# Routing attention and a bilinear feed-forward layer on one core: eight small moves in a hand-written order of work

## The chip, the cores and the metric

The kernel runs on one core of a Trainium2 chip. A core has five engines, each with its own instruction stream that it works through in order: TensorE (PE in the profile, with the loading of its weights as PEld), VectorE (DVE), ScalarE (ACT), GpSimd (POOL) and SyncE (SP, which here only issues DMAs). Work on one engine waits for work on another through semaphores. The metric is the device time of one execution in microseconds (us).

## What is computed

Attention with routing (4 batches, 8 heads, 768 positions, 64 wide, 16 centroids to a head), and a feed-forward layer on its output (3072 tokens, 512 wide, 1536 inside):

```python
q_n, k_n, c_n = (t / (norm(t) + 1e-6) for t in (q, k, centroids))
q_assign = argmax(einsum('bhsd,hcd->bhsc', q_n, c_n))
k_assign = argmax(einsum('bhsd,hcd->bhsc', k_n, c_n))
mask = q_assign[:, :, :, None] == k_assign[:, :, None, :]
scores = where(mask, q @ k.T / sqrt(64), -1e9)
x = softmax(scores) @ v               # regrouped to (3072, 512)
out = ((x @ w_a) * (x @ w_b)) @ w_out # weights come as 64-bit floats
```

## The kernel before, in words

**Attention.** Two heads of one batch make a *pair* p (0 to 15; HP = 4 pairs to a batch, so that pair 4 is the first of batch 1). A pair has two halves hf of 384 query positions, a half has six key blocks j, and one key block of one half is a *unit*. The loop at the end of `short_path` runs over *groups* g of two units: six groups to a pair, 96 in all, and l = g % 6 is the group's place in its pair. In each group the following is issued, in this order: the scores of group g (`score`: TensorE L556, then the exponential on ScalarE, L565); the sums of the exponentials of the group before, which become the softmax's denominators (`add_up`, L586, on VectorE or GpSimd); the last step of a weight's rounding (`flush_w`, L302, VectorE); the products with v of the group before (`weigh`, L597); in every third group the products that sum the denominators across partitions (`denominators`, L620, copied out by ScalarE, L625); one preparing step of the next pair (`ready[l]()`); the rounding of a weight (`round_w`, four VectorE instructions L280 to L290, then GpSimd L295), where one is due; and then as many *pieces* of the feed-forward layer as a credit allows. After each piece one entry of the list `todo` is issued, and then another rounding if one is due. What is left in `todo` comes at the end of the group.

**What `todo` holds.** Small VectorE steps: a half's normalisation (`normalize`: transposition L640, reciprocal L643, transposition L647, and the product L652 that scales x, which is on GpSimd), and for pairs from 4 on (`by_blocks`) the steps of the next pair's routing. These are, by l: the transpositions of q and k (L477), the transposition of the similarities out of the accumulator that `prep_sim` has just filled (L481; the products are TensorE L373), the maxima (L502 to L507), the one-hots (L487 on GpSimd, L489 on VectorE) and their transposition (L493). Once the feed-forward layer has begun, so from pair 5's preparation (g = 25) on, the accumulator of `prep_sim` is one of the two that the next group's scores need (`apart()`).

**The feed-forward layer.** Batch 0 is computed with plain products (`ffn_block`): its first 8 pieces, which need x of pair 3's first half, are put into the list `ffn` at g = 22. Batches 1 to 3 use a scheme of seven products in place of eight (`ffn_ups`, then `ffn_downs`). It needs sums and differences of blocks of x (`combine_x`, L755, six VectorE instructions; `combine_t4`, L767) and of the weights (`combine`, L782: S1, S2 as `half_1`, S3, S4 as `half_2`, two instructions each). A *part* is one block of one weight: the products p1, p2, p6, p5, p7, p3, p4 in this order, 12 parts to a batch. Every product has eight matmuls (L678), and its result is added up by VectorE (`add`, L815; L864 in p4) or copied by ScalarE (`take`, L812). A part uses three accumulators X, Y and Z; the next part's Y is the same accumulator as this one's, so the next part's p2 has to wait until this part's p3 has been added up. `half_1` of the next part is issued after p7's own steps, and `half_2` after p4's. The last products of `ffn_downs` add up their results at L939. `combine_x` is put into `ffn` in front of the last two of these (`FREE_ROOM` = 2); the next batch's p1 and p2 follow them.

**The beginning.** 24 matmuls at L1053 and 12 transpositions of the identity (`keep_busy`, L332) run while the first q and k arrive. Pair 0's twelve blocks of q and k are transposed in three calls i = 0, 1, 2 of `prep_transpose` (L354), and copied out of the accumulators by VectorE (L360, L363) or ScalarE (L361, L365). In between, the centroids are transposed (L321) and copied (L322, L325), and `prep_sim(0)` (L373) needs them.

Of the kernel before, what the change touches and what calls it, by code (L numbers as in the profile page):

```python
# [14 lines left out]
ALU = mybir.AluOpType  # L15
# [123 lines left out]
def short_path(nc, tc, ctx, c, cn, centroids_in, casts, n_far, q, k, v,  # L139
# [3 lines left out]
    B, H, S, D = q.shape  # L143
# [3 lines left out]
    HP = H // 2  # L147
# [3 lines left out]
    HB = S // 2  # L151
# [177 lines left out]
    def keep_busy(n):  # L329

        for _ in range(n):
            nc.tensor.transpose(out=idle[:, 0:P], in_=ident, identity=ident)  # L332
# [15 lines left out]
    def prep_transpose(p, i):  # L348
        if i == 0:
            qkTs[p] = qtp.tile([P, 2 * S], FP32, name="qkT")  # L350
        ps = ps_m.tile([P, 512], FP32, name="m")
        for n in range(4):
            w, j = divmod(4 * i + n, NJ)
            nc.tensor.transpose(  # L354
                out=ps[:, n * P:(n + 1) * P],
                in_=qks[p][:, w, j].rearrange("p a d -> p (a d)"),
                identity=ident)
        dst = qkTs[p][:, i * 512:(i + 1) * 512]
        if p == 0 and i == 2:
            nc.vector.tensor_copy(out=dst[:, 0:256], in_=ps[:, 0:256])  # L360
            nc.scalar.copy(out=dst[:, 256:], in_=ps[:, 256:])  # L361
        elif p == 0 and i != 1 or p == 1 and i == 2:
            nc.vector.tensor_copy(out=dst, in_=ps)  # L363
        else:
            nc.scalar.copy(out=dst, in_=ps)  # L365
# [148 lines left out]
    def prep_steps(p):  # L514
        if p >= NPAIR:
            return [lambda: None] * 6

        def both(*fs):
            return lambda: [f() for f in fs]

        if by_blocks(p):
            steps = prep_by_blocks(p)
            ready = [lambda s=s: todo.extend(s) for s in steps]
            ready[1] = both(lambda: prep_sim(p), lambda: load_v(p), ready[1])
            return ready

        return [
            lambda: p > 1 and (prep_transpose(p, 0), prep_transpose(p, 1)),
            both(lambda: prep_sim(p), lambda: load_v(p)),
            lambda: todo.extend(prep_assign(prep_across(p))),  # L530
            lambda: None,
            lambda: prep_onehot(p, 1),
            lambda: None,
        ]
# [41 lines left out]
    def add_up(u):  # L576
        p, hf, j = where(u)
        if j == 0 or j == NJ - 1 and p < HP:
            return
        if j == 1:  # L580
            accs[p, hf] = accp.tile([P, 2, HB], FP32, name="acc")
        acc = accs[p, hf]
        for a in range(2):
            many = p >= HP and (a == 1 or j in (2, 4))
            eng = nc.gpsimd if many else nc.vector
            eng.tensor_tensor(  # L586
                out=acc[:, a, :],
                in0=probs[u - 1][:, a, :] if j == 1 else acc[:, a, :],
                in1=probs[u][:, a, :], op=ALU.add)
# [39 lines left out]
    def normalize(p, hf):  # L629

        b, hp = divmod(p, HP)
        acc = den_of.pop((p, hf))
        den, once = acc[:, 0, :], acc[:, 1, :]
        x = xTs[b][:, hp, hf * HB:(hf + 1) * HB]
        inv = small.tile([P, HB // 32], FP32, name="inv")

        def across():
            nc.vector.transpose(out=once, in_=den)  # L640

        def invert():
            nc.vector.reciprocal(  # L643
                out=inv, in_=once.rearrange("p (j t) -> p j t", t=32)[:, :, 0])

        def back():
            nc.vector.transpose(  # L647
                out=den,
                in_=inv[:, :, None].broadcast_to((P, HB // 32, 32)))

        def apply():
            nc.gpsimd.tensor_tensor(out=x, in0=x, in1=den, op=ALU.mult)  # L652
            unchecked.append((4 * p + 2 * hf + 1, inv))

        return [across, invert, back, apply]
# [88 lines left out]
                      chunks(comb.rearrange("p (c f) -> p c f", c=2)),  # L744
                      [t[:, HB:] for t in size]]

    def combine_x(b):
        up_room()
        x = xTs[b]
        for c in range(2):  # L750
            x11, x12 = x[:, c, 0:HB], x[:, c, HB:S]
            x22 = x[:, c + 2, HB:S]
            t2, t3 = W["T2"][c], W["T3"][c]
            for out, l, r in ((t3, x22, x12), (x12, x12, x11), (t2, x22, x12)):
                nc.vector.tensor_tensor(out=out, in0=l, in1=r, op=ALU.subtract)  # L755

    def ffn_ups(b, h):

# [11 lines left out]
        def products(w_sb, i, is_a):  # L770
# [11 lines left out]
                    nc.vector.tensor_tensor(out=dst[c], in0=l[c], in1=r[c], op=op)  # L782
                A[name] = dst

            def half_1():
                combine("S1", A["21"], A["22"], ALU.add)
                combine("S2", A["S1"], A["11"], ALU.subtract)

            def half_2():
                combine("S3", A["11"], A["21"], ALU.subtract)  # L790
                combine("S4", A["12"], A["S2"], ALU.subtract)
                s = W["slots"]
                W["slots"] = [s[0], s[2], s[1], s[3]]
# [70 lines left out]
                nc.vector.tensor_tensor(out=to, in0=to, in1=box["X"][:, 0:HB],  # L864
                                        op=ALU.mult)

            return half_1, half_2, [p1, p2, p6, p5, p7, p3, p4]

        parts = [products(w_sb, i, w_sb is wa_sb) for i in range(NF // 2)
                 for w_sb in (wa_sb, wb_sb)]  # L870
        pieces = []
        for n, (half_1, half_2, ps) in enumerate(parts):
            if n == 0:
                ps[0] = both(half_1, half_2, ps[0])
                ps[2] = both(combine_t4, ps[2])
            if n + 1 < len(parts):
                ps[4] = both(ps[4], parts[n + 1][0])
                ps[6] = both(ps[6], parts[n + 1][1])
            pieces += [(2 * HB, f) for f in ps]
        return pieces  # L880

# [124 lines left out]
    def both(*fs):  # L1006
        return lambda: [f() for f in fs]
# [3 lines left out]
    def ffn_ready(p, hf):  # L1011

        b, hp = divmod(p, HP)
        if hp < HP - 1:
            return
        if b > 0:
            if hf == 0:
                return
            h = []
            ffn.insert(len(ffn) - FREE_ROOM, (0, lambda: combine_x(b)))  # L1020
            ffn.extend(ffn_ups(b, h) + ffn_downs(b, lambda: h))
        elif hf == 0:
            blocks[0] = ffn_block(0, 0)
            ffn.extend(blocks[0][0][0:8])
        else:
            ups0, box0 = blocks[0]
            ups, box = ffn_block(0, 1)
            for n in range(3):
                ffn.extend(ups[8 * n:8 * n + 8] + ups0[8 * n + 8:8 * n + 16])
            ffn.extend(ffn_downs(0, lambda: (box0["h"], box["h"])))  # L1030
# [21 lines left out]
    for _ in range(12):  # L1052
        nc.tensor.matmul(out=idle[0:D, 0:D], lhsT=ones, rhs=ones, start=True,  # L1053
                         stop=True)
    keep_busy(12)
    prep_transpose(0, 0)
    prep_transpose(0, 1)
    centroids_across()
    prep_transpose(0, 2)
# [24 lines left out]
    for g in range(NG + 3):  # L1084
        p, l = divmod(g, GPP)
        if l == 0:
            ready = prep_steps(p + 1)
        now = (2 * g, 2 * g + 1)
        before = (2 * g - 2, 2 * g - 1)
        if g == 1:  # L1090
            weigh(before)
        if 0 < g < NG:
            score(now)
        check_inverses()
        if 0 < g <= NG:
            for u in before:
                add_up(u)
        flush_w()
        if 1 < g <= NG:
            weigh(before)  # L1100
        late = int(g > EARLY)
        if g % 3 == late and 0 < g - late:
            denominators(*divmod(g // 3 - 1, 2))
        if g < NG:
            ready[l]()
        parts = due.get(g, [])

        def round_next():
            if parts:
                i = parts.pop(0)  # L1110
                round_w(i)
                load_w(i + 2)

        round_next()
        if g <= EARLY:
            first, second = 4, 1
        else:
            first, second = 5, 3 if g < NG else 2
        ph = {first: (p, 0), second: (p - 1, 1)}.get(l)
        halved = ph in den_of  # L1120
        if halved:
            todo.extend(normalize(*ph))
        if ffn:
            credit += PER_GROUP[(g > 2 * BG + 3) + (g > 3 * BG + 3)]
            least = FREE_ROOM if halved and ph[1] and (ph[0] + 1) % HP == 0 else 0
            while len(ffn) > least and credit > 0:
                cost, piece = ffn.popleft()
                credit -= cost
                piece()
                if todo:  # L1130
                    todo.popleft()()
                round_next()
        else:
            credit = 0
        round_next()
        while todo:
            todo.popleft()()
        if halved:
            ffn_ready(*ph)
        if l == 0 and p + 1 < NPAIR:  # L1140
            if p and not by_blocks(p + 1):
                prep_transpose(p + 1, 2)
            load(p + 2)
        if l == 4 and p + 1 < NPAIR and not by_blocks(p + 1):
            prep_onehot(p + 1, 0)
# [248 lines left out]
```

## Time and profile before

| what | value |
|---|---|
| median of nine runs | 1048.04 us (1047.7 to 1048.74) |
| the profiled execution | 1047.8 us |
| its span, first to last instruction | 1045.6 us |
| mean granted TensorE clock | 0.999 |
| TensorE busy | 1033.0 us, 99% |
| VectorE busy | 657.2 us, 63% |
| GpSimd busy | 329.8 us, 32% |
| ScalarE busy | 303.2 us, 29% |
| chain that ended last | PE 93%, DVE 4%, issue 1%, POOL 1% |

The span lies within the execution's time; the 2.2 us between them lie around it. "Busy" counts instructions that run or wait in the engine's pipe: for TensorE the end of a matmul is modelled, so that a short pause between matmuls can hide in it. In the timeline a line gives start, length, engine, line of code, operation, output and inputs, the number of merged instructions, and in brackets how long the engine had been idle before and what released it.

### The profile page before, as it was taken

To read this page: it belongs to the slowest core of one execution; us is meant where nothing else is said; L and a number is where in the kernel's file an instruction comes from. 1 tells how busy PE (TensorE), PEld (TensorE's weight loads), DVE (VectorE), ACT (ScalarE), POOL (GpSimd) and SP (SyncE) were. 2 spreads that over 40 slices of the span, in tenths; PEclk is the share of its full clock that TensorE was granted. 3 is DMA by queue.
4 is the path that set the end of the run, shared out by engine and by line. 5 is a ranking of instruction groups with operands and counts; after the bars stand their busy time and mean duration, and the time that the engine had idled before them with its cause. 6 is when DMAs were issued, how large, how long until landed. Compare 5 with 4: busy or idle time off the path is not lost.

```text
span 1045.6 us, 17833 instructions
## 1 busy us (share of the span) xinstructions
PE 1033.0 (99%) x7163; PEld 502.7 (48%) x7163; DVE 657.2 (63%) x1314; ACT 303.2 (29%) x590; POOL 329.8 (32%) x311
## 2 busy tenths in 40 slices
PE   9999999999999999999999999999999999999997
PEld 5444444444445554444444555444444565444565
DVE  6778877887857447555556746755454845554652
ACT  5665333233322222333322122233232201111100
POOL 1111345455543323343442422443333310211100
PEclk9999999999999999999999999999999999999999
DMA  7334243526230120203020030300000000000001
GB/s 183 87 86 86 85 107 105 122 70 145 63 50 18 41 44 22 39 5 46 4 46 2 25 67 24 47 1 20 1 4 1 11 31 21 1 1 1 1 31 34
DMA packets 120521, 46.48 MB, mean 44 GB/s; under 512 B 106608, under 2 KB 115824, under 8 KB 120432
## 3 DMA queue, kind: packets, MB, share of 16 engines
q1 hardware_dynamic: 120016, 44.85, 18.8%
q8 instruction: 58, 0.95, 0.4%
q10 hardware_dynamic: 416, 0.43, 0.1%
q14 instruction: 31, 0.25, 0.1%
HBM read 37.78 MB, written 6.29 MB: 42 GB/s over the span
## 4 chain that ended last, share of the span: by engine, by line
PE 93%; DVE 4%; issue 1%; POOL 1%; ACT 0%; DMA 0%; DVEq 0%; POOLq 0%
PE m L678 62%; PE s L556 15%; PE O L597 12%; PE s L620 1%; PE s L373 1%; PE m L620 1%; DVE raw L755 1%; PE m L373 0%; POOL xT L652 0%; DMA h<-in_q_dram 0%; DVE xT L755 0%; PE m L354 0%; DVE comb L782 0%; DVE acc L586 0%; DVE acc L647 0%
## 5 line engine op out<-in xcount | busy, mean ns | idle before, releaser
L565 ACT ACTIVATE pt<-s 128x768 f32<-128x768 f32 x192 | 145.3, 808 | 206.5 <-PE s L556 165.0
L586 POOL TENSOR_TENSOR acc<-acc,pt 128x384 f32<-128x384 f32 x144 | 152.5, 1073 | 60.2 <-ACT pt L565 43.0
L597 PE MATMUL O<-pt,v 128*64 128x384 f32 x768 | 145.0, 499 | 0.0
L556 PE MATMUL s<-qkT 64*128 64x384 f32 x768 | 139.7, 482 | 0.0
L821 POOL TENSOR_TENSOR h<-h,ha 128x384 f32<-128x384 f32 x54 | 55.4, 1029 | 258.7 <-DVE ha L815 257.8
L678 PE MATMUL m<-xT,wa_sb 128*64 128x384 f32 x672 | 117.5, 487 | 2.8 <-DVE ha L815 1.0
L678 PE MATMUL m<-xT,wb_sb 128*64 128x384 f32 x672 | 116.9, 487 | 0.0
L815 DVE TENSOR_TENSOR ha<-ha,m 128x384 f32<-128x384 f32 x72 | 39.6, 550 | 98.0 <-PE m L678 75.4
L586 DVE TENSOR_TENSOR acc<-acc,pt 128x384 f32<-128x384 f32 x96 | 74.5, 802 | 36.5 <-POOL acc L586 35.5
L815 DVE TENSOR_TENSOR h<-h,m 128x384 f32<-128x384 f32 x72 | 39.5, 549 | 80.8 <-PE m L678 53.9
L812 ACT COPY h<-m 128x384 f32<-128x384 f32 x72 | 34.5, 479 | 184.9 <-PE m L678 184.9
L597 PEld LDWEIGHTS O<-pt,v 128*64 128x64 f32 x768 | 46.7, 136 | 85.8 <-issue 80.1
L678 PE MATMUL m<-wo_sb,h 128*64 128x256 f32 x768 | 86.7, 379 | 0.0
L556 PEld LDWEIGHTS s<-qkT 64*128 64x128 f32 x768 | 70.5, 187 | 31.3 <-issue 0.2
L678 PEld LDWEIGHTS m<-xT,wa_sb 128*64 128x64 f32 x672 | 48.7, 137 | 63.4 <-issue 53.3
L678 PE MATMUL m<-raw 128*64 128x384 f32 x432 | 78.9, 486 | 0.0
L652 POOL TENSOR_TENSOR xT<-xT,acc 128x384 f32<-128x384 f32 x32 | 32.9, 1027 | 144.9 <-DVE acc L647 144.8
L678 PEld LDWEIGHTS m<-xT,wb_sb 128*64 128x64 f32 x672 | 49.0, 137 | 60.1 <-issue 56.1
L678 PEld LDWEIGHTS m<-wo_sb,h 128*64 128x64 f32 x768 | 55.0, 137 | 31.0 <-issue 5.0
L678 PE MATMUL m<-xT,h 128*64 128x256 f32 x576 | 64.5, 379 | 0.0
L678 PE MATMUL m<-xT,size 128*64 128x384 f32 x288 | 52.7, 487 | 0.0
L678 PEld LDWEIGHTS m<-xT,h 128*64 128x64 f32 x576 | 41.4, 137 | 22.3 <-issue 2.3
(169 smaller groups left out, 1302.3 us busy)
## 6 DMA issues: line engine op xcount, KB each, us to landing
raw<-in_moe_w_a_dram SPq DMA_DIRECT2D x12, 512.0 KB, 3.9
raw<-in_moe_w_b_dram SPq DMA_DIRECT2D x12, 512.0 KB, 3.7
raw<-in_moe_w_out_dram SPq DMA_DIRECT2D x12, 512.0 KB, 3.7
qk<-in_q_dram SPq DMA_DIRECT2D x48, 96.0 KB, 3.1
qk<-in_k_dram SPq DMA_DIRECT2D x48, 96.0 KB, 3.6
v<-in_v_dram SPq DMA_DIRECT2D x24, 192.0 KB, 3.9
out_dram<-rest SPq DMA_DIRECT2D x24, 128.0 KB, 1.7
v<-in_v_dram SPq DMA_DIRECT2D x4, 384.0 KB, 4.5
```

The costliest lines, as they stand in the source:

```text
L373: nc.tensor.matmul(out=ps[32 * kq:32 * kq + 32, 0:HB], lhsT=cTb[:, hp, :], rhs=qkTs[p][:, kq * HB:(kq + 1) * HB], start=True, stop=True)
L556: nc.tensor.matmul(out=s[:, a, 0:HB], lhsT=Ts[p][r, S + j * P:S + (j + 1) * P], rhs=Ts[p][r, hf * HB:(hf + 1) * HB], start=start, stop=not ...
L565: nc.scalar.activation(out=pt, in_=s[:, :, 0:HB], func=AF.Exp, scale=SCALE)
L586: eng.tensor_tensor(out=acc[:, a, :], in0=probs[u - 1][:, a, :] if j == 1 else acc[:, a, :], in1=probs[u][:, a, :], op=ALU.add)
L597: nc.tensor.matmul(out=O_of[0][a * D:(a + 1) * D, 0:HB], lhsT=vs[p][:, a, j, :], rhs=probs[u][:, a, :], start=(j == 0), stop=(j == NJ - 1))
L620: nc.tensor.matmul(out=ps[a * D:(a + 1) * D, 0:HB], lhsT=ones, rhs=t[:, a, :], start=(n == 0), stop=(n == len(terms) - 1))
L652: nc.gpsimd.tensor_tensor(out=x, in0=x, in1=den, op=ALU.mult)
L678: nc.tensor.matmul(out=ps[half], lhsT=lhsT[:, half], rhs=rhs, **kw)
L755: nc.vector.tensor_tensor(out=out, in0=l, in1=r, op=ALU.subtract)
L812: nc.scalar.copy(out=box[name], in_=box["X"][:, 0:HB])
L815: nc.vector.tensor_tensor(out=box[name], in0=box[name], in1=box[bank][:, 0:HB], op=ALU.add)
L821: nc.gpsimd.tensor_tensor(out=to, in0=to, in1=box[name], op=ALU.mult)
```

## The change

Eight edits, in the order of the code:

1. The first pair's copies: i = 0 goes from VectorE to ScalarE, and i = 2, which the two engines shared, goes to VectorE alone. (Pair 1 keeps its copies.)
2. The similarities' transposition (L481) leaves `todo` and is issued at once, after `prep_sim` and the load of v.
3. Of a half's sums for a = 0, VectorE does j = 1, 2, 3 and GpSimd j = 4, 5; before, VectorE did j = 1, 3, 5 and GpSimd j = 2, 4. The sums for a = 1 stay on GpSimd.
4. The scaling of x for pair 3's first half is done by VectorE and no longer by GpSimd.
5. `combine_x` is cut into two pieces of three instructions; the second is put between the last two products of `ffn_downs`.
6. The combinations of weights come in three steps: S1 after p7, S2 after p3, S3 and S4 after p4.
7. Of the 12 `keep_busy` transpositions at the beginning, 5 stay, and 2 come after the first call of `prep_transpose`.
8. The denominators of pair 3's second half are put into `ffn`, behind the first piece of group 24.

```diff
-        if p == 0 and i == 2:
-            nc.vector.tensor_copy(out=dst[:, 0:256], in_=ps[:, 0:256])
-            nc.scalar.copy(out=dst[:, 256:], in_=ps[:, 256:])
-        elif p == 0 and i != 1 or p == 1 and i == 2:
+        if p < 2 and i == 2:
             nc.vector.tensor_copy(out=dst, in_=ps)
         else:
             nc.scalar.copy(out=dst, in_=ps)
...
-            ready[1] = both(lambda: prep_sim(p), lambda: load_v(p), ready[1])
+            ready[1] = both(lambda: prep_sim(p), lambda: load_v(p), steps[1][0],
+                            lambda: todo.extend(steps[1][1:]))
...
-            many = p >= HP and (a == 1 or j in (2, 4))
+            many = p >= HP and (a == 1 or j > 3)
...
-            nc.gpsimd.tensor_tensor(out=x, in0=x, in1=den, op=ALU.mult)
+            eng = nc.vector if (p, hf) == (HP - 1, 0) else nc.gpsimd
+            eng.tensor_tensor(out=x, in0=x, in1=den, op=ALU.mult)
...
-    def combine_x(b):
-        up_room()
+    def combine_x(b, c):
+        if c == 0:
+            up_room()
         x = xTs[b]
-        for c in range(2):
...
-            def half_1():
+            def first():
                 combine("S1", A["21"], A["22"], ALU.add)
+
+            def second():
                 combine("S2", A["S1"], A["11"], ALU.subtract)
 
-            def half_2():
+            def others():
...
-                ps[4] = both(ps[4], parts[n + 1][0])
-                ps[6] = both(ps[6], parts[n + 1][1])
+                for i, step in enumerate(parts[n + 1][0], 4):
+                    ps[i] = both(ps[i], step)
...
-            ffn.insert(len(ffn) - FREE_ROOM, (0, lambda: combine_x(b)))
+            for c in range(2):
+                ffn.insert(len(ffn) - FREE_ROOM + c, (0, lambda c=c: combine_x(b, c)))
...
-    keep_busy(12)
+    keep_busy(5)
     prep_transpose(0, 0)
+    keep_busy(2)
     prep_transpose(0, 1)
...
-            denominators(*divmod(g // 3 - 1, 2))
+            half = divmod(g // 3 - 1, 2)
+            if half == (HP - 1, 1):
+                ffn.insert(1, (0, lambda: denominators(HP - 1, 1)))
+            else:
+                denominators(*half)
```

More of the change, by code (lines that the diff above doesn't have):

```diff
@@ L745, in up_room @@
                       [t[:, HB:] for t in size]]
-    def combine_x(b):
-        up_room()
+    def combine_x(b, c):
+        if c == 0:
+            up_room()
         x = xTs[b]
-        for c in range(2):
[L751 to L755, printed above, removed]
+        x11, x12 = x[:, c, 0:HB], x[:, c, HB:S]
+        x22 = x[:, c + 2, HB:S]
+        t2, t3 = W["T2"][c], W["T3"][c]
+        for out, l, r in ((t3, x22, x12), (x12, x12, x11), (t2, x22, x12)):
+            nc.vector.tensor_tensor(out=out, in0=l, in1=r, op=ALU.subtract)
     def ffn_ups(b, h):
@@ L865, in p4 @@
                                         op=ALU.mult)
-            return half_1, half_2, [p1, p2, p6, p5, p7, p3, p4]
+            return (first, second, others), [p1, p2, p6, p5, p7, p3, p4]
         parts = [products(w_sb, i, w_sb is wa_sb) for i in range(NF // 2)
@@ L871, in ffn_ups @@
         pieces = []
-        for n, (half_1, half_2, ps) in enumerate(parts):
+        for n, (combinations, ps) in enumerate(parts):
             if n == 0:
-                ps[0] = both(half_1, half_2, ps[0])
+                ps[0] = both(*combinations, ps[0])
                 ps[2] = both(combine_t4, ps[2])
             if n + 1 < len(parts):
-                ps[4] = both(ps[4], parts[n + 1][0])
-                ps[6] = both(ps[6], parts[n + 1][1])
+                for i, step in enumerate(parts[n + 1][0], 4):
+                    ps[i] = both(ps[i], step)
             pieces += [(2 * HB, f) for f in ps]
```

## The prediction

> **What bounds the kernel.** I read the page's shares first, then TensorE's waits, then the timeline around each.
>
> ```profile
> PE 1033.0 (99%) x7163; PEld 502.7 (48%) x7163; DVE 657.2 (63%) x1314; ACT 303.2 (29%) x590; POOL 329.8 (32%) x311
> ```
>
> TensorE is the bound. No edit removes any of its matmuls but five idle transpositions, so a gain can only be time in which TensorE waits. Its waits, all but the first 1.1 us and three small ones of the start:
>
> ```profile
> PE m L678 <- DVE ha L815: 1.0, 2, 0.5
> PE s L556 <- DVE sim L481: 1.0, 1, 1.0
> PE m L678 <- POOL xT L652: 0.9, 1, 0.9
> PE m L678 <- DVE rest L939: 0.9, 2, 0.4
> PE m L373 <- DVE cTb L325: 0.6, 1, 0.6
> PE s L620 <- DVE acc L586: 0.5, 1, 0.5
> ```
>
> Total, times, longest. They are idle time after a modelled end, so the loss is larger. I measure it by starts: the chain of waits has 32 L678 matmuls in 5.16 us, 0.161 each; a run of n that is followed later than n x 0.161 has lost the rest.
>
> **The change part by part.**
>
> *Combinations of x in two parts (5).*
>
> ```profile
> 396.54 0.57 DVE oh L493
> 397.11 0.32 DVE rest L939
> 397.42 0.04 issue
> 397.47 1.51 PE m L678 x8
> ```
>
> This is the chain that ended last. p1 starts at 395.57, p2 could at 396.86 and does at 397.47: 0.61 lost, because the last products' sum (L939) stands behind six L755 (390.24 to 396.6). With three ahead (to 392.9, then L493, 0.57) it runs at about 393.5, right after its product's end (393.15). The other three, 2.4 us at most beside GpSimd's sums, end near 396.2, and the next L939 near 396.6; its accumulator is wanted only after p2 and p6. The same at 646.42 (0.60); batch 3 loses nothing there. **-1.2 us**.
>
> *Combinations of weights one at a time (6).*
>
> ```profile
> 505.67 1.31 DVE L782 TENSOR_TENSOR comb<-wa_sb 128x128 f32<-128x128 f32 x2
> ...
> 508.43 0.54 DVE L815 TENSOR_TENSOR ha<-ha,m 128x384 f32<-128x384 f32 x1
> ...
> 509.02 1.51 PE L678 MATMUL m<-xT,wa_sb 128*64 128x384 f32 x8 [0.51 <-DVE ha L815]
> ```
>
> In the timeline, p1 of the next part starts at 507.05, so p2 could start at 508.34: 0.68 lost, as at 757.97. p3's sum (508.43) is behind S1, S2 (506.91 to 508.04) and a one-hot (L489). With S2 behind it, it starts 1.05 earlier, at 507.4, and ends at 507.95; what is next is 0.35 us of slack. S2 is wanted by p6, a product later and two attention steps on. **-1.35 us**.
>
> *Denominators behind a product (8).* From 122.07 to the scores at 129.78 TensorE has 40 matmuls (6.45 us, 0.1 for the change of kind) and takes 7.71: 1.16 lost, since acc is only summed at 123.3 and the two halves of the array then run out of step until 129.4. A product of 2.58 in front covers that. Its accumulator is free; the exit copy (L625) is over long before the next scores. **-1.15 us**.
>
> *Similarities put across at once (2)* has two sides.
>
> ```profile
> 136.64 0.56 DVE L709 TENSOR_TENSOR h<-ha,m 128x384 f32<-128x384 f32 x1 [3.66 <-PE m L678]
> 137.11 0.58 DVE L481 STREAM_TRANSPOSE sim<-s 128x384 f32<-128x384 f32 x1
> ...
> 137.75 0.34 PE L556 MATMUL s<-ohT 64*128 64x384 bf16 x2 [0.95 <-DVE sim L481]
> ```
>
> The gain: at g = 25 the scores wait for L481, which waits behind a piece's product. A pair of L556 in bf16 takes 0.17, and the first started at 136.46, so TensorE could go on at 136.63: 1.12 lost. The similarities are there at 133.8, and VectorE is idle for 3.66 us before 136.64: L481 then ends near 134.4, two microseconds before the scores. Rounding (2.25, below) moves behind it and ends about when L709 is due. **-1.1 us**.
>
> The loss: `ready[l]()` comes before `round_next()`, so L481 now stands *in front of* a due rounding and holds it until the similarities exist. At g = 19 this matters:
>
> ```profile
> 95.83 0.58 DVE L481 STREAM_TRANSPOSE sim<-m 128x384 f32<-128x384 f32 x1 [2.41 <-PE m L373]
> ...
> 101.98 1.02 DVE L586 TENSOR_TENSOR acc<-acc,pt 128x384 f32<-128x384 f32 x2
> 102.59 1.33 PE L620 MATMUL m<-acc,ones 128*64 128x384 f32 x4
> ```
>
> TensorE's L373 runs from 94.91; before 95.83 VectorE is idle for 2.41 us, with the rounding done from 91.09 to 93.42. The rounding falls behind 96.34; its price is the step of the same four instructions from 104.91 to 107.16, 2.25 us. From 95.83 on VectorE has no pause (11.63 busy of 12.20 us from 95.8 to 108), so L586 comes at 104.2, and the denominators, which already lose 0.45 here (two waits of 0.23), lose 2.25 more. GpSimd's L295 and the one-hots queue behind it, all as late. **+2.25 us**. At g = 31 the same order costs VectorE 1.1 us of waiting (free at 191.08, similarities done 192.2), and L709 still meets its product's end: nothing. Bounds for this edit's later pairs: from no loss to 2.25 for g = 37 as well; taken: none.
>
> *Scaling on VectorE (4).* Piece 1 starts at 110.07; its 12 matmuls end at 112.00, the rest wait until 113.05 for L652 on GpSimd: 1.05 lost. VectorE's product of this shape takes 0.55 (L586, 0.56 for one) and follows L647 (ends 111.70) with no handover; GpSimd's took 0.17 to begin and 1.13. So x is there near 112.3. It moves L586 of the next sums back by 0.5, which the missing contention returns (four took 2.73 there, two take 1.02). **-0.7 us**, bounded by -1.05 (the whole wait) and 0 (the handover is no dearer than VectorE's queue); the late chain of g = 19 shifts both sides alike.
>
> *VectorE's sums first (3).* The same number of sums on each engine. VectorE loses its waits on GpSimd (DVE acc L586 <- POOL acc L586: 35.5 us, 18 times), none on TensorE's path. GpSimd has two sums in a half's middle group and four in the last, 4.3 us against 3.2. Denominators come a group later: the closest is 849.86, 3.52 after the last sum (846.34); 2.4 stay. **0**; bounds: -0.5 (a sum of p3 that gets clear) to +2 (three places like 509.02).
> [...]
>
> *First pair (1, 7).* The chain runs q's landing, VectorE's chain for the centroids, L322, L325, L373. Without i = 0's copy L322 starts at 7.11, when L321 has ended, not 7.20. The last L373 waits now for ScalarE's half of i = 2 (8.47 to 8.85, starts at 8.90); VectorE alone copies from 7.93 to 8.62 (0.69, row of L363), so it starts at 8.66. ScalarE is free for i = 0 at 6.23 and for i = 1 at 6.85. **-0.2 us**; bounds -0.6 (TensorE's wait for L325) to +1.4: the idle transpositions run at two paces, three of L332 from 3.83 to 4.53 (0.23 apart), twelve of L354 at 40.87 in 1.46 (0.12); if the change of pace came late, the first pair's 13 would cost 0.11 more each.
> [...]
>
> **Sum.** -1.2 - 1.35 - 1.15 - 1.1 + 2.25 - 0.7 - 0.2 = -3.45. From the profiled 1047.8 (0.24 under the median of 1048.04): 1044.35, say **1044.4 us**.
>
> **Rivals.**
> - *The late rounding is caught up* (g = 19): if VectorE's order lets L586 through, -5.7: 1042.1. For it: only the code's order says otherwise. Against: no idle time on VectorE until 107.7.
> - *VectorE's lag goes on* into the first pieces: it is 13.56 busy of 16 us from 114 to 130. Then the denominators and the scores of g = 26 wait for it still, and 2.25 of gains go: 1046.6. Against: denominators want acc near 126.8, and with 2.1 us of lag it is there at 125.5.
> - *The start misses its pace*: +1.4 and no -0.2: 1045.9, on the border.
> - *Slower: GpSimd's four sums hold up p3's sum.* Place: L782 and one step of `todo` between p7's sum and p3's. With ScalarE's copy 0.7, L815 0.55, S1 1.31, a step at 1.36 and L815 0.55 the chain has 4.46 us for three products, 3.87: 0.6 a part. Six of 36 parts eat the gain; from ten on it is slower. Twelve: 1044.4 + 7.2 = 1051.6. For it: two places did this before. Against: S2's 0.5 to 1.1 has left that chain.
> - *It does nothing*: TensorE's short waits come back at the next accumulator. That has the lag's price.
>
> **Numbers.** Forecast 0.55, caught up 0.12, lag 0.18, pace 0.08, slower 0.07. 0.2% of 1048.04 is 2.1 us, about what a measurement can tell from none: faster is under 1045.9. The forecast, the first rival and a part of the pace's make 0.71; same, with the lag and the pace's rest, 0.22; slower 0.07. The range leaves out the slower rival and the edges: 1042.0 to 1047.0.
>
> **What would show it.** Right: no wait on L939, L652's is gone or 0.3, none on L481; p2 straight behind p1; one new wait of TensorE at L620 near 102 us, for VectorE's acc, of about 2.3; L280 behind L481 at g = 19. Wrong: that wait absent, new waits of L678 for L815, or L620 waiting for GpSimd.

## The result, and the profile after

The changed kernel takes 1044.98 us, the median of 10 runs (1043.89 to 1045.6), against 1048.07 for the kernel before in 30 runs (1047.39 to 1048.87). The ratio is 0.9968, 95% interval 0.996 to 0.9976: faster by 3.1 us, where 3.6 was forecast. The profiled execution took 1043.79 with a span of 1042.1, 4.0 less than the profiled 1047.8 of before.

One thing has to be known about these times: they have two levels. Six of twelve executions had a mean granted TensorE clock of 0.997 and average 1045.26; six had 0.998 or more and average 1044.00. The profiled one is of the second kind. Why there are two levels is one of the findings below.

First the shares on the page:

```profile
span 1042.1 us, 17904 instructions
...
PE 1030.8 (99%) x7158; PEld 500.1 (48%) x7158; DVE 658.8 (63%) x1314; ACT 303.0 (29%) x590; POOL 334.1 (32%) x310
```

The span fell by 3.6, and TensorE has the same instructions but for the five idle transpositions, so the gain is waiting time. (Its busy time fell by 2.2, since a short pause between matmuls counts as busy.) TensorE's waits (total, times, longest):

```profile
PE m L619 <- DVE acc L585: 2.1, 1, 2.1
PE O L1057 <- DVE ones L80: 1.1, 1, 1.1
PE m L370 <- DVE cTb L325: 0.5, 1, 0.5
PE m L447 <- DVE oh L421: 0.4, 2, 0.3
PE m L679 <- DVE raw L910: 0.3, 1, 0.3
PE m L447 <- ACT qkT L362: 0.3, 1, 0.3
PE m L679 <- DVE xT L653: 0.2, 1, 0.2
```

The waits for L815, L481, L652's scaling on GpSimd and L939 are gone (L939 is L942 now, L815 is L818). Two are new: 2.1 for `acc` at L619, which was forecast, and 0.3 for L910, which was not; the 0.2 for L653 is what is left of the wait for the scaling. The timeline around the first:

```profile
94.40 0.85 PE L370 MATMUL m<-qkT,cTb 128*32 128x384 f32 x8
95.32 0.58 DVE L478 STREAM_TRANSPOSE sim<-m 128x384 f32<-128x384 f32 x1 [4.66 <-PE m L370]
95.82 0.39 DVE L280 TENSOR_SCALAR wa_sb<-raw 128x512 int32<-128x512 int32 x1
...
103.72 1.02 DVE L585 TENSOR_TENSOR acc<-acc,pt 128x384 f32<-128x384 f32 x2
104.32 1.33 PE L619 MATMUL m<-acc,ones 128*64 128x384 f32 x4 [2.10 <-DVE acc L585]
```

VectorE stands idle for 4.66 us before the similarities' transposition (2.41 before the change), with the due rounding (L280) behind it, and pays that back at 103.72, where TensorE waits. Three of the gains, each as one line of the timelines: VectorE's scaling of x with the wait that is left, the product moved in front of p2 of the next part, and p3's sum (L818) in front of S2 (the L783 behind it).

```profile
114.08 0.87 PE L679 MATMUL m<-xT,wa_sb 128*64 128x384 f32 x4 [0.17 <-DVE xT L653]
...
393.91 2.75 PE L679 MATMUL m<-xT,wa_sb 128*64 128x384 f32 x16
...
505.13 0.54 DVE L818 TENSOR_TENSOR ha<-ha,m 128x384 f32<-128x384 f32 x1
505.60 0.66 DVE L783 TENSOR_TENSOR raw<-comb,wa_sb 128x128 f32<-128x128 f32 x2
```

p1 and p2 at 393.91 are one run of 16 matmuls without a gap; before, the second eight followed 0.61 late.

**Where the time went, by steps.** TensorE works through a fixed list, so I take the start of each group's scores (the first L556 of group g, now L554) in both profiles and look where the difference changes:

| place | before | after | step | edit, forecast |
|---|---|---|---|---|
| g = 0, counted from the first L227 | 6.22 | 6.00 | -0.22 | 1 and 7: -0.2 |
| g = 22 | 103.85 | 105.58 | +2.25 | 2: +2.25 |
| g = 24 | 119.01 | 120.04 | -0.70 | 4: -0.7 |
| g = 25 | 129.78 | 129.65 | -1.16 | 8: -1.15 |
| g = 27 | 151.06 | 149.81 | -1.13 | 2: -1.1 |
| g = 38 | 255.2 | 253.54 | -0.40 | none |
| g = 53 and 77 | 398.91, 647.86 | 396.6, 644.82 | -0.66, -0.65 | 5: -1.2 |
| g = 64 and 88 | 510.46, 759.41 | 507.42, 755.64 | -0.73, -0.73 | 6: -1.35 |
| g = 71 | 581.99 | 579.6 | +0.65 | 3: 0 |

In this execution L227, which waits for q's landing, itself came 0.28 earlier. With that and 0.2 lost at the very end the steps make the span's 3.57. The time outside the span is 1.7 instead of 2.2; that gives the other 0.5 of the profiled difference.

### The profile page after: what moved, and what is told of

Same layout as the page of the kernel before. It is cut to its first block, busy times and chain, and to the rows that moved or that the text cites. A ratio compares the mean times of both kernels' runs of the same rounds, so it can differ in the third digit from the quotient of the medians.

```text
span 1042.1 us, 17904 instructions
## 1 busy us (share of the span) xinstructions
PE 1030.8 (99%) x7158; PEld 500.1 (48%) x7158; DVE 658.8 (63%) x1314; ACT 303.0 (29%) x590; POOL 334.1 (32%) x310
## 4 chain that ended last, share of the span: by engine, by line
PE 95%; DVE 2%; issue 1%; POOL 0%; DMA 0%; ACT 0%; DVEq 0%; POOLq 0%
PE m L679 63%; PE s L554 15%; PE O L596 13%; PE s L619 2%; PE m L619 1%; PE s L370 1%; PE m L370 0%; PE m L354 0%; DMA h<-in_q_dram 0%; DVE xT L910 0%; DVE raw L910 0%; PE m L430 0%; POOL xT L653 0%; PE m L384 0%; DVE h L919 0%
## 5 line engine op out<-in xcount | busy, mean ns | idle before, releaser
L585 POOL TENSOR_TENSOR acc<-acc,pt 128x384 f32<-128x384 f32 x144 | 155.6, 1101 | 60.0 <-ACT pt L563 45.9
L554 PE MATMUL s<-qkT 64*128 64x384 f32 x768 | 139.7, 483 | 0.0
L824 POOL TENSOR_TENSOR h<-h,ha 128x384 f32<-128x384 f32 x54 | 56.0, 1040 | 255.6 <-DVE ha L818 255.2
L818 DVE TENSOR_TENSOR ha<-ha,m 128x384 f32<-128x384 f32 x72 | 39.7, 551 | 106.5 <-PE m L679 80.4
L815 ACT COPY h<-m 128x384 f32<-128x384 f32 x72 | 34.5, 479 | 184.9 <-PE m L679 181.5
L554 PEld LDWEIGHTS s<-qkT 64*128 64x128 f32 x768 | 70.5, 187 | 31.3 <-issue 0.2
L818 DVE TENSOR_TENSOR h<-h,m 128x384 f32<-128x384 f32 x72 | 39.5, 549 | 72.3 <-PE m L679 46.9
L653 POOL TENSOR_TENSOR xT<-xT,acc 128x384 f32<-128x384 f32 x31 | 32.4, 1046 | 143.1 <-DVE acc L646 143.1
L585 DVE TENSOR_TENSOR acc<-acc,pt 128x384 f32<-128x384 f32 x96 | 63.4, 687 | 2.3 <-ACT pt L563 1.0
```

Source lines behind the costliest of these rows:

```text
L554: nc.tensor.matmul(out=s[:, a, 0:HB], lhsT=Ts[p][r, S + j * P:S + (j + 1) * P], rhs=Ts[p][r, hf * HB:(hf + 1) * HB], start=start, stop=not ...
L585: eng.tensor_tensor(out=acc[:, a, :], in0=probs[u - 1][:, a, :] if j == 1 else acc[:, a, :], in1=probs[u][:, a, :], op=ALU.add)
L653: eng.tensor_tensor(out=x, in0=x, in1=den, op=ALU.mult)
L815: nc.scalar.copy(out=box[name], in_=box["X"][:, 0:HB])
L818: nc.vector.tensor_tensor(out=box[name], in0=box[name], in1=box[bank][:, 0:HB], op=ALU.add)
L824: nc.gpsimd.tensor_tensor(out=to, in0=to, in1=box[name], op=ALU.mult)
```

## The experiments

Each edit is to the changed kernel unless another is named. "Step" is the difference as in the table.

**The sums' order (3).** `e1_sums_back` undoes edit 3 alone:

```diff
-            many = p >= HP and (a == 1 or j > 3)
+            many = p >= HP and (a == 1 or j in (2, 4))
```

> The changed kernel with edit 3 undone: VectorE sums j = 1, 3, 5 again and GpSimd j = 2, 4. Theory: the new loss of 0.65 us of TensorE before the scores of group 71 comes from GpSimd's four sums in a row, which hold VectorE's one-hot (0.55 us before, 1.21 after); undone, the loss goes, and the 0.40 us gained before the scores of group 38 (VectorE free earlier for the transposition of q and k) goes too: 0.25 us faster, at most 0.7. Rival: the loss at group 71 comes from the order of the pieces; it stays, and the kernel is 0.4 us slower.

1044.76 us (1044.47 to 1045.94, 7 runs), ratio to before 0.9971 [0.996, 0.9982]. In medians nothing shows, but three steps move: 0.65 comes back at g = 71, 0.79 is lost at g = 38 and 0.14 at g = 32. By the steps e1 is 0.28 slower than the changed kernel, where 0.25 faster was expected. (The 0.79 is more than the 0.40 that the whole change gains there; e5, below, says where the rest is from.)

The gain at g = 38 begins one group earlier. Before the change, VectorE waits for GpSimd's sum (L586); from there it has no pause until the transposition of q and k (L477), and the second half of TensorE's L373 waits for that:

```profile
241.84 1.34 DVE L586 TENSOR_TENSOR acc<-acc,pt 128x384 f32<-128x384 f32 x1 [2.10 <-POOL acc L586]
247.23 1.83 DVE L477 STREAM_TRANSPOSE qkT<-qk 128x768 f32<-128x768 f32 x2
248.70 1.25 PE L373 MATMUL s<-qkT,cTb 128*32 128x384 f32 x8
249.11 0.14 PEld L373 LDWEIGHTS s<-qkT,cTb 128*32 128x32 f32 x4 [0.27 <-DVE qkT L477]
```

In the changed kernel VectorE does not wait there, the transposition (L474) ends before L370 begins, and L370 has no pause:

```profile
244.96 1.82 DVE L474 STREAM_TRANSPOSE qkT<-qk 128x768 f32<-128x768 f32 x2
247.44 0.85 PE L370 MATMUL s<-qkT,cTb 128*32 128x384 f32 x8
```

What happens at g = 71 is on VectorE too. In the changed kernel's timeline GpSimd does this:

```profile
559.66 3.88 POOL L585 TENSOR_TENSOR acc<-acc,pt 128x384 f32<-128x384 f32 x4
563.62 1.04 POOL L484 TENSOR_TENSOR oh<-sim,first 64x384 bf16<-64x384 f32 x1
```

VectorE in the same stretch, and 12 us on:

```profile
562.75 1.21 DVE L486 TENSOR_TENSOR oh<-sim,first 64x384 bf16<-64x384 f32 x1
...
574.55 3.98 DVE L910 TENSOR_TENSOR raw<-wo_sb 128x512 f32<-128x512 f32 x3
```

And TensorE, with the wait at its end:

```profile
578.58 1.08 PE L679 MATMUL m<-raw,ha 128*64 128x256 f32 x8 [0.32 <-DVE raw L910]
```

And VectorE of `e1_sums_back` at the same one-hot and the same L910:

```profile
562.28 1.34 DVE L585 TENSOR_TENSOR acc<-acc,pt 128x384 f32<-128x384 f32 x1 [2.10 <-POOL acc L585]
564.40 0.54 DVE L486 TENSOR_TENSOR oh<-sim,first 64x384 bf16<-64x384 f32 x1
...
575.85 3.69 DVE L910 TENSOR_TENSOR raw<-wo_sb 128x512 f32<-128x512 f32 x3
```

With four sums in a row on GpSimd, L486 takes 1.21 us, with three 0.54 (0.55 before the change). From there the lag stays in the chain up to L910. The chain goes once through GpSimd, for whose scaling of x VectorE waits 1.18 us in both kernels; beside that `e1_sums_back` has only 0.20 us of idle time in it, and its three L910 take 3.69 us and not 3.98. Counted from the product that begins at 562.05 (563.72 in `e1_sums_back`), L910 ends 0.66 us later, and TensorE waits.

**The loss of edit 2.** `e2_first_sims_late` leaves only pair 4's similarities on the list, and has the later pairs' issued at once:

```diff
-            ready[1] = both(lambda: prep_sim(p), lambda: load_v(p), steps[1][0],
-                            lambda: todo.extend(steps[1][1:]))
+            if p == HP:
+                ready[1] = both(lambda: prep_sim(p), lambda: load_v(p), ready[1])
+            else:
+                ready[1] = both(lambda: prep_sim(p), lambda: load_v(p),
+                                steps[1][0])
```

> The changed kernel with pair 4's similarities put across from the list again, behind the rounding, and at once only from pair 5 on. Theory: the new wait of 2.25 us at the denominators of group 21 is VectorE's idle time in front of that one transposition; it goes and nothing else moves: 2.25 us faster. Rival: VectorE is the bound up to the scores of group 26, and part of the time comes back as a wait there: 1 us faster or less.

1041.99 us (1041.88 to 1043.03, 5 runs), ratio 0.9944 [0.9931, 0.9958]. VectorE at the place:

```profile
95.89 0.58 DVE L478 STREAM_TRANSPOSE sim<-m 128x384 f32<-128x384 f32 x1 [2.41 <-PE m L370]
```

The idle time is 2.41 again as before the change, with the rounding in front; TensorE's wait at L619 is gone, and so is the step of 2.25. No other step moves. The order on VectorE was the whole cause. (By the medians the kernel is 3.0 faster than the changed one, and 2.0 below the mean of that one's runs at full clock.)

**The two levels of the clock.** The prediction saw a danger at the start: a late change of pace. `e3_twelve` puts all 12 in front again, `e4_none` takes all away:

```diff
-    keep_busy(5)
+    keep_busy(12)
     prep_transpose(0, 0)
-    keep_busy(2)
```

```diff
-    keep_busy(5)
     prep_transpose(0, 0)
-    keep_busy(2)
```

> The changed kernel with edit 7 undone: 12 idle transpositions in front, none behind the first block. The runs of the changed kernel with a mean granted clock of 0.997 took 1045.26 us on average, those with 0.998 to 1.000 took 1044.00. Theory: with five transpositions the full clock comes late in about half of the executions; with twelve all runs are of the quick kind, near 1044.1, and the median is 0.8 us lower. Rival: the clock's beginning has nothing to do with the number; the same two kinds, median 1045.0.

> The changed kernel without any idle transposition in front of or behind the first block (the 24 small matmuls stay). Theory of the pace: the clock comes late in all or nearly all executions, granted 0.997 or below, 1045.3 us or more. Rival: nothing changes, or 0.1 us is gained at the first block: 1044.9.

With twelve: 1044.91 (1044.04 to 1046.02, 8 runs), and four of the eight at a clock of 0.997 still. The start does not differ: 6.00 us from L227 to the first scores, as with five and two. With none: 1045.51 (1043.8 to 1046.8, 8 runs), 6.64 in its profile, 0.64 worse, and two runs at 0.995 (why is not known), two at 0.997. So the two levels don't come from having fewer transpositions at the start, and edit 7 neither gains nor loses.

The start has a spread of its own. Idle transpositions and those of the first pair follow each other 0.21 us apart until the clock rises, and 0.11 apart from then on. That is at 5.04 us in the changed kernel's profile. In the profile of e7 (below), which has the same start, it is at 6.86, and the first scores come 0.34 later; in that of e5 (below), which has the old start with all twelve, it is at 7.09, and they come 0.54 later than in the kernel before.

`e5_sims_alone` is the kernel before with edit 2 alone, to price it by itself:

```diff
-            ready[1] = both(lambda: prep_sim(p), lambda: load_v(p), ready[1])
+            ready[1] = both(lambda: prep_sim(p), lambda: load_v(p), steps[1][0],
+                            lambda: todo.extend(steps[1][1:]))
```

> The kernel before with edit 2 alone. Theory: the scores of group 26 come 1.1 us earlier, the denominators of group 21 2.25 us later, and the denominators of group 24, which are not behind a product here, wait for VectorE as before: about +1.1 us in all, 1049.2. If TensorE's idle time of 2 us at group 21 is what lets the clock fall back in some executions, then some of these runs show a granted clock of 0.997 and 1.3 us more, which no run of the kernel before shows. Rival: edit 2 is a gain by itself.

1049.81 (1049.41 to 1050.3, 11 runs), ratio 1.0015 [1.0006, 1.0024]. Its profile happens to catch a run at 0.997. Stretch, length, busy time (and instructions) of PE, PEld, DVE, ACT and POOL, granted clock, DMA share, GB/s:

```profile
101.00:106.00 5.00, 2.90 (x17) 0.96 (x14) 4.97 (x10) 2.15 (x5) 1.12 (x1) 1.00 0.24 91
106.00:109.50 3.50, 3.50 (x14) 1.43 (x14) 3.40 (x8) 0.58 (x2) 0.00 (x0) 0.51 0.00 0
109.50:114.00 4.50, 4.50 (x30) 1.86 (x28) 2.34 (x6) 3.17 (x5) 2.36 (x2) 1.00 0.26 58
```

After TensorE's 2.1 us of waiting the clock stands at half for some 3.4 us, which fill nearly all of the second stretch, and comes back. What it costs there shows in the matmuls behind the wait, which take 1.33 and 0.50 us at full clock:

```profile
105.65 2.01 PE L621 MATMUL m<-acc,ones 128*64 128x384 f32 x4 [2.10 <-DVE acc L587]
107.59 0.82 PE L557 MATMUL s<-ohT 64*128 64x384 bf16 x4
```

By steps the half clock costs 1.60 us in this profile (0.68 at g = 22, beside edit 2's 2.25, and 0.92 at g = 23). But 1.58 comes back at g = 24 and 25, where TensorE had waited for GpSimd's scaling and for VectorE's sum before: it now arrives late enough not to wait. So the price depends on what waits stand behind. The four runs of this kernel at 0.997 average 0.5 more than its others, and not the 1.3 that was expected. In the changed kernel's own profile, the stretch behind the same wait has 1.00:

```profile
104.30:107.70 3.40, 3.38 (x20) 1.45 (x22) 3.33 (x7) 1.46 (x4) 0.00 (x0) 1.00 0.00 0
```

So the same 2.1 us of waiting stood before a half clock (0.51) in one profile and before a full one (1.00) in the other.

`e7_filled` keeps the wait and fills it with idle transpositions ahead of g = 21's denominators:

```diff
+            if g == 21:
+                fill = ps_m.tile([P, 512], FP32, name="m")
+                for _ in range(18):
+                    nc.tensor.transpose(out=fill[:, 0:P], in_=ident, identity=ident)
```

> The changed kernel with 18 idle transpositions (about 2 us) in front of the denominators of group 21, where TensorE waits for VectorE's sum, so that it is busy and not idle there. Theory of the clock: six of twelve runs of the changed kernel had a granted clock of 0.997 and took 1.26 us more because the idle time lets the clock fall back; filled, all runs are of the quick kind, median 1044.1, at most 1044.7. Rival: the slow kind has nothing to do with that wait; about half of the runs stay above 1044.9.

1044.25 (1043.98 to 1045.25, 5 runs), with clocks of 0.998 and 0.999 only. The run of 1045.25 is over the 1044.7 expected at most, at a clock of 0.999; e1, e2, e5, e9 and e10 have one such run each, 0.6 to 1.2 above the median of their others at full clock, and where that time goes is not known. TensorE:

```profile
102.21 2.18 PE L1112 MATMUL m<-ident 128*128 128x128 f32 x18
...
105.03 1.33 PE L619 MATMUL m<-acc,ones 128*64 128x384 f32 x4
```

The step of +2.25 is unchanged, since L619 waits for `acc` as long as before, but TensorE is busy meanwhile. Over all kernels: with this wait open (the changed kernel, e1, e3, e4, e5 and e8) 20 of 57 executions have 0.997 or less; without it, or with it filled (e2, e6, e7, e9, e10, e11), none of 30, and none of the 46 of the kernel before beside them. That the clock falls because of this wait is shown by one profile and these counts; 5 runs of the filled kernel alone would be few.

**Edit 2 alone** also answers how the later pairs stand. The seven runs of `e5_sims_alone` at full clock have a median of 1049.53 (1049.41 to 1050.11), 1.5 above before, where +2.25 - 1.1 makes 1.15. Its steps show two more losses, 0.14 at g = 32 and 0.43 at g = 38, where L373 waits longer for the transposition of q and k (it takes 1.60 us, 1.25 before): later pairs' similarities cost VectorE time too. In the whole change edit 3 pays for them, as e1 shows by bringing them back.

**The denominators (8).** `e8_den_back` undoes edit 8 alone:

```diff
-            half = divmod(g // 3 - 1, 2)
-            if half == (HP - 1, 1):
-                ffn.insert(1, (0, lambda: denominators(HP - 1, 1)))
-            else:
-                denominators(*half)
+            denominators(*divmod(g // 3 - 1, 2))
```

> The changed kernel with edit 8 undone: the denominators of pair 3's second half in front of the product again. Theory: VectorE is 1.9 us later than in the kernel before when it comes to their sum, while TensorE is 1.0 us later; so the wait is 0.8 to 0.9 us longer than the 1.16 us that it cost before, and the kernel is 2.0 us slower than the changed one. Rival: the edit is worth 1.16 us here too.

1045.88 (1045.56 to 1046.18, 11 runs), 0.9 above the changed kernel by medians, and 1.9 above its mean at full clock. The step at g = 25 is +0.58 instead of -1.16, so edit 8 is worth 1.74 here: more than forecast, because edit 2's lag makes `acc` later: TensorE's wait is 1.05 us, 0.48 in the kernel before. The one run of the eleven at 0.997 is the fastest of them, so the lower clock costs nothing that shows in this kernel.

```profile
125.42 1.00 PE L619 MATMUL s<-acc,ones 128*64 128x384 f32 x3 [1.05 <-DVE acc L585]
```

**A better version.** `e6_sums_by_half` is e2 with edit 3 only in a pair's second half (`hf` is 1), and the old order in the first:

```diff
-            many = p >= HP and (a == 1 or j > 3)
+            many = p >= HP and (a == 1 or (j > 3 if hf else j in (2, 4)))
```

> The variant with pair 4's similarities in the list (1041.99 us), and VectorE's sums in front of GpSimd's only in second halves, since the one-hot of the first halves' groups stands right behind GpSimd's four sums. Theory: the 0.65 us at group 71 goes and the 0.40 us at group 38 stays: 1041.3. Rival: the gain at group 38 comes from the first halves as well, and both go: 1041.7. No run at a granted clock of 0.997, since no wait at group 21 is left.

1041.68 (1041.47 to 1041.93, 5 runs), ratio 0.9938 [0.9924, 0.9952]: 3.3 under the changed kernel, 6.4 under the one before. The step at g = 71 is gone and the -0.40 at g = 38 is kept. Against e2 the medians differ by 0.3 where the step says 0.65: from the start of the last matmul to the end e6's profile takes 6.85 us, e2's 6.36. By their times the two are not told apart. (The sums that matter for g = 38 are those of a second half, the ones that hold up g = 71 those of a first.)

Three kernels take edits back out of e6. They ran on another chip, where the kernel before took 1048.27 and not 1048.05, so some 0.2 of each difference to e6 is the chip's. `e9_combos_back` has edits 5 and 6 undone, each combination in its old place:

```diff
-                for i, step in enumerate(parts[n + 1][0], 4):
-                    ps[i] = both(ps[i], step)
+                one, two, three = parts[n + 1][0]
+                ps[4] = both(ps[4], one, two)
+                ps[6] = both(ps[6], three)
...
-            for c in range(2):
-                ffn.insert(len(ffn) - FREE_ROOM + c, (0, lambda c=c: combine_x(b, c)))
+            ffn.insert(len(ffn) - FREE_ROOM,
+                       (0, lambda: [combine_x(b, c) for c in range(2)]))
```

> The best variant so far (1041.68 us, no wait at group 21) with edits 5 and 6 undone: the combinations of x in one piece, those of weights in two steps. Theory: the four waits of 0.60 to 0.68 us at the parts' second products come back, two for L939's accumulator and two for L815's, and the four steps of 0.65, 0.65, 0.73 and 0.73 that the changed kernel gained are theirs: 2.6 to 2.8 us slower, 1044.4. Rival: part of the steps belongs to VectorE's freedom from GpSimd's sums (edit 3), and at least one wait stays away: 1043.8 or less.

1043.07 (1042.65 to 1044.23, 5 runs), 1.4 above e6. TensorE waits where edit 6's two places are, and 0.72 comes back at g = 64 and at g = 88:

```profile
PE m L682 <- DVE ha L821: 1.0, 2, 0.5
```

There is no wait of TensorE on the last products' sum (now L946). The two steps of edit 5 don't come back. VectorE:

```profile
392.05 0.56 DVE L759 TENSOR_TENSOR raw<-xT 128x384 f32<-128x384 f32 x1
392.53 0.57 DVE L490 STREAM_TRANSPOSE oh<-oh 128x384 bf16<-128x384 bf16 x1
393.02 0.38 DVE L946 TENSOR_TENSOR rest<-rest,m 128x256 f32<-128x256 f32 x1
```

All six combinations in one piece end at 392.6, where before they ended at 396.6; 3.2 of that is the lead that TensorE has here by then, and the rest is VectorE's own: the six take 5.55 us from the first start to the last end and not 6.38. In this order GpSimd does three sums beside them instead of four, and a combination takes 1.24 to 1.36 us beside a sum and 0.56 without. Edit 2 alone does not remove the two waits (e5 has both). So, as far as these runs show, edit 3's order removes them without edit 5; and in e1, which has edit 5 and not edit 3's order, they are gone as well: either edit is enough. (No run has the rest of the change without both.)

`e10_scaling_back` gives GpSimd the scaling back (edit 4 undone in e6), `e11_sims_listed` puts all similarities' transpositions back on the list (edit 2 undone in e6):

```diff
-            eng = nc.vector if (p, hf) == (HP - 1, 0) else nc.gpsimd
-            eng.tensor_tensor(out=x, in0=x, in1=den, op=ALU.mult)
+            nc.gpsimd.tensor_tensor(out=x, in0=x, in1=den, op=ALU.mult)
```

> The best variant so far with edit 4 undone: pair 3's first half is scaled by GpSimd. Theory: 0.7 us slower, 1042.4: the wait before the scores of group 24 is 1.05 and not 0.34. Rival: without the late rounding of group 19 the denominators of group 21 and the scaling have slack of their own, and it costs nothing.

1042.6 (1042.25 to 1043.7, 5 runs), 0.9 above e6; the step at g = 24 is +0.70, by this wait:

```profile
PE m L681 <- POOL xT L655: 0.9, 1, 0.9
```

```diff
-            if p == HP:
-                ready[1] = both(lambda: prep_sim(p), lambda: load_v(p), ready[1])
-            else:
-                ready[1] = both(lambda: prep_sim(p), lambda: load_v(p),
-                                steps[1][0])
+            ready[1] = both(lambda: prep_sim(p), lambda: load_v(p), ready[1])
```

> The best variant so far with edit 2 undone for all pairs: the similarities from the list again. Theory: only the wait before the scores of group 26 comes back, 1.13 us, 1042.8; the gain at group 38 is edit 3's and stays. Rival: at groups 32 and 38, where edit 2 alone cost 0.14 and 0.43, edit 2 costs TensorE time here too, and without it the kernel is only 0.5 us slower.

1042.78 (1042.4 to 1042.96, 5 runs), 1.1 above e6; the step at g = 27 is +1.12:

```profile
PE s L553 <- DVE sim L478: 1.0, 1, 1.0
```

## Why the prediction was right

The sign, the size and the mechanism held. By its own steps:

- **Combinations of x, -1.2**: measured -1.31. But the price is not edit 5's own: e9 shows that edit 3 takes the same waits away. The step cut six instructions in two against GpSimd's sums as they had been, and did not look at what edit 3 does to those sums. It would have been wrong as a price for edit 5 alone in a kernel that has edit 3.
- **Combinations of weights, -1.35**: measured -1.46, and +1.44 in e9 when undone. Its own.
- **Denominators, -1.15**: measured -1.16. That the two halves run out of step after the wait, and that the loss is larger than the wait, was in this term. In the trace of the kernel before, the two matmuls of a pair start 0.006 us apart up to 122.40, and from 123.83 to 129.04 the starts follow each other 0.15 and 0.18 apart in turn (with one at 0.10 and one at 0.23 at the beginning). e8 agrees on the price: a wait of 0.48 costs 1.16 in the kernel before and one of 1.05 costs 1.74 in e8, some 0.7 more than the wait both times.
- **Similarities at once, -1.1 and +2.25**: measured -1.13 and +2.25. The bound for later pairs, taken as none, hid 0.57: e5 shows it at g = 32 and 38 when edit 2 is alone. In the whole change it does not appear, since edit 3 freed VectorE there.
- **Scaling on VectorE, -0.7**: measured -0.70, and e10 +0.70.
- **Sums first, 0**: here two sizes were off, in both directions. GpSimd's four sums were weighed at one place, p3's sum at 508, and it is not held there: L818 starts at 505.13 and takes 0.54. But four sums in a row also lie beside one-hots (L486), at g = 71 in front of a chain without slack: +0.65, as e1 shows. The step checked the place that was already late, and not the places that had no slack left. And VectorE's waits on GpSimd, "none on TensorE's path", did have one: at g = 37 VectorE's wait for GpSimd's sum ran through L477 to TensorE's L373, which took 1.25 us before and 0.85 after. That is the -0.40.
- **First pair, -0.2**: measured -0.22 from L227 on, and e3 has the same with twelve transpositions, so it is edit 1's. When q lands differs between executions from 4.27 to 5.02 us, three times the term, and a late rise of the clock costs as much again (0.34 in e7's profile).

The terms that had a price add up to -3.73 as measured, against -3.45; the two misses of edit 3 (+0.65 and -0.40) bring it to -3.48. From the profiled 1047.8 the forecast's 1044.35 is 0.35 over the mean of the runs at full clock (1044.00), and 0.6 under the median, since half the runs lose 1.26 more by the clock. That the sum came out so near is in part luck: the two misses of edit 3 nearly cancel, and neither the half clock nor the 0.5 us outside the span, which work against each other, was in a term.

Of the rivals: *caught up* is out, since L280 stood behind L478 and the step was 2.25. *The lag goes on* is out: the gains at g = 25 and 27 came in full. *The start misses its pace* saw a danger at the start, but what goes with the longer half of the runs is a lower clock (0.997 or less in 20 of 57 executions with the new wait at L619 open, in none of 30 without), which e5's profile shows as a fall behind that wait, and the late rise that some profiles show at the start is in e5 too, which has all twelve transpositions. The price of the new wait is therefore 2.25 in some runs of the changed kernel and 3.5 in the others. *GpSimd's four sums hold up p3's sum* had the right cause with a wrong victim: at one place out of all, a one-hot. *It does nothing* is out: behind the steps of the table no gain is lost again up to the last scores.

Open: the 0.5 us outside the span (1.7 to 1.9 in each variant of the changed kernel, 2.2 in the kernel before and in e5). e3 has 1.8, so edit 7 is not the cause; which of the others is was not tried. Also open is why the same 2.1 us of waiting lowers the clock in some executions and not in others. In three traces the times at which the granted clock changes lie whole multiples of 3.413 us apart: 1034.24 us (303) from 5.04 to 1039.28 in the changed kernel's, 1037.65 (304) from 4.94 to 1042.59 in that of the kernel before, 98.99 (29) and 3.41 (1) in e5's, where it is full from 7.09 and half from 106.08 to 109.49. In e5's the wait lies wholly in one such stretch, 102.67 to 106.08, of which TensorE is busy for 38%; in the changed kernel's it lies across two, busy for 47% and 91%, and the clock stays at 1.00. An estimate from these lengths: a wait of 2.10 at a random place falls wholly into one stretch of 3.41 in 38% of executions, and 20 of 57 are 35%. One profile with a fall is too few to call this shown.

## What to carry to other kernels

When an instruction is moved ahead of a list, look at what else is due at that point, and price the idle time of the engine *in front of it*: 2.25 us were read off before the run, from the timeline alone, and one condition brings them back. An edit that reorders work on one engine changes the prices of the other edits on that engine, so a price taken from the old profile belongs to the set of edits and not to one of them. Look for places without slack as well as for places that are late: the loss came where nothing had been waiting.

## What the runs showed of the hardware

- Behind a wait of 2.1 us on TensorE its clock stood at half for some 3.4 us in e5's profile (0.51 in 106 to 109.5) and at 1.00 in the changed kernel's; with this wait open 20 of 57 executions have a mean clock of 0.997 or less, without it none of 30. The cost is 1.60 us on the spot in e5's profile, 1.26 in the mean of the changed kernel, and next to nothing where later waits take it up (1.58 of the 1.60 in e5's profile). With eighteen idle transpositions in the wait (2.18 us) the mean clock was 0.998 or 0.999 in five of five runs.
- A comparison of two inputs on VectorE (the one-hot, 64x384, with a bf16 result) takes 0.54 us, and 1.21 beside the fourth of GpSimd's sums in a row, while the four sums take 3.88, 0.97 each. In the kernel before, three took 3.23 at the same place, 1.08 each. At this one place VectorE has the delay, and GpSimd none that shows.
- Twelve, seven or no idle transpositions at the start: 6.00, 6.00 and 6.64 us from L227 to the first scores, in one profile each (and 6.34 in e7's, with seven).
